# Two heads per tile and batched gathering in a decode attention kernel

## The chip, the cores and the metric

The kernel runs on one core of a Trainium2 chip. The time is device microseconds of that core, from launch to end. Three runs of the kernel before took 393.71, 392.96 and 393.02 us; their median, 393.02 us, is what the change is compared with. A separate profiled execution took 393.22 us; inside it the profile sees 391.4 us from the first to the last instruction (the span).

The core has a matrix engine (TensorE, PE in the profile, with weight loads listed apart as PEld), a vector engine (VectorE, DVE), a scalar engine (ScalarE, ACT), GpSimd (POOL) and a sync engine (SyncE, SP), which here only issues transfers. Sixteen DMA engines move data between the main memory (HBM) and the on-chip memory (SBUF). Matrix products land in a second on-chip memory, PSUM.

## The reference

One token is decoded: `x` is one row of 512 numbers. After a layer norm, two branches run on it and both are added to `x`.

```python
xn = layernorm(x)
# A: attention over a cache of 4096 keys, 32 heads of 128
q = (xn @ wq).reshape(32, 128)
scores = einsum("hd,hkd->hk", q, k_cache) * 128 ** -0.5
p = softmax(scores)
o = einsum("hk,hkd->hd", p, v_cache)
a = o.reshape(4096) @ wo
# B: SwiGLU, 512 -> 1376 -> 512, scaled by a router's sigmoid, plus xn
y = (silu(xn @ w_gate) * (xn @ w_up)) @ w_down * sigmoid(xn @ w_r)
out = x + a + (xn + y)
```

All of it is float32. The two caches hold 32 x 4096 x 128 numbers each, 67.1 MB; `wq` and `wo` are 8.4 MB each and the three matrices of branch B 2.8 MB each. Every weight and cache entry is used once.

## The kernel before

**Loads.** One pool of 12 slots of 128 x 4096 floats (2 MB, 16 KB per partition) takes every weight and cache tile in turn, so a load waits until the tile that held its slot twelve loads earlier has been used up. All of these loads go through SP's queue, in the order `wq` (4 loads), `w_gate`, `w_up` (2 each), K of head 0, then K of head g and V of head g-1 alternately, then `wo` (8 loads of 1 MB) and `w_down` (3 loads and a last one for 96 rows that are left over). One head's keys, 4096 x 128, lie as 128 partitions x 32 keys (chunks) x 128.

**Scores.** Loop round g does head g's scores and the rest of head g-1. Of head g's 32 chunks, VectorE multiplies 12 with the head's query in two bulk instructions (`multiply`, L281), in place, and ScalarE sums each of these chunks with an instruction of its own (`sums`, L288). The other 20 are done by VectorE with a fused multiply-and-sum, one instruction and a read-out of its accumulator per chunk (`dots`, L292). The query has to stand on all 128 partitions; a matrix product with a row of ones copies it there, once per head (`q_group`, L222).

**Softmax and values.** For head g-1, VectorE takes each partition's maximum and spreads it over a diagonal (`own_max`, L299 and L301), TensorE mixes the partitions (L303), VectorE takes the head's maximum (`head_max`, L308) and ScalarE the exponentials with their sums (`expo`, L315). TensorE sums these sums over the partitions (`denominators`, L183), and multiplies exponentials with V: 16 products of 2 chunks each, in four column groups of the array (`values`, L332). ScalarE copies the result out of PSUM (`gather`, L340). Eight products with a selection matrix pick the four column groups' parts, add them, and turn the row of 128 into a column layout (`collect`, L354); ScalarE scales by the inverse of the denominator (L359). Every fourth head VectorE copies the four heads' results to a tile of their own (`keep`, L365).

**Branch B** runs while the first keys arrive: two products with `w_gate` and `w_up` (L238), sigmoid, and 41 small products that turn the hidden row into columns (L267, L269).

**The end.** 172 products (`accumulate`, L372) multiply all heads' results with `wo` and the hidden columns with `w_down`, all into one PSUM tile, in the order of the loads. VectorE adds the residual (L418), and SP stores the row (L419).

The order on every engine is the order in which the code is written; no scheduler moves anything. A float32 matrix product is two passes on TensorE, each with a weight load and a multiplication of its own, so each of the 1152 products in the code gives four instructions (2304 PE and 2304 PEld in the profile).

Of the kernel before, what the change touches and what calls it, by code (L numbers as in the profile page):

```python
# [14 lines left out]
HP = 1  # L15
SLOTS = 12
NA = 12
G = 2
# [3 lines left out]
NJ = 10  # L22


@with_exitstack
def kernel(
# [21 lines left out]
    GB = HB // HP  # L48
# [4 lines left out]
    QC = 512  # L53
    SLOT = C * Dh
    EPS = 1e-5
# [7 lines left out]
    ps_s = ctx.enter_context(tc.tile_pool(name="ps_s", bufs=3, space=bass.MemoryType.PSUM))  # L63
# [3 lines left out]
    def slot(name):  # L67
        return stream.tile([P, SLOT], F32, name="slot")

    def load_wq():  # L70
        rows = SLOT // (H * Dh)
        src = wq.rearrange("(p j) n -> p (j n)", p=P)
        WQ = []
        for i in range(0, NK, rows):
            t = slot("wq")
            nc.sync.dma_start(t, src[:, i * H * Dh:(i + rows) * H * Dh])
            WQ += [t[:, j * H * Dh:(j + 1) * H * Dh] for j in range(rows)]
        return WQ

    def load_in(w):  # L80
        rows = min(NK, SLOT // F)
        src = w.rearrange("(p j) f -> p (j f)", p=P)
        W = []
        for i in range(0, NK, rows):
            t = slot("w_in")
            n = rows * F
            nc.sync.dma_start(t[:, :n], src[:, i * F:i * F + n])
            W += [t[:, j * F:(j + 1) * F] for j in range(rows)]
        return W

    def load_cache(cache, g):
        t = slot("kv")
# [4 lines left out]
    def load_wo():  # L97
        W = []
        n = SLOT // (RB * D)
        for b in range(0, H // HB, n):  # L100
            t = slot("wo").rearrange("p (b r n) -> p b (r n)", b=n, n=D)
# [8 lines left out]
    def load_down():  # L110
        src = w_down[:FM, :].rearrange("(p j) n -> p j n", p=P)
        rows = SLOT // D
        W = []
        if rows > NJ:
            t = slot("w_down").rearrange("p (j n) -> p j n", n=D)
            parts = [(t, 0, 5), (t, 5, 3), (t, 8, 2)]
            last = t[:, NJ]
        else:
            t = slot("w_down").rearrange("p (j n) -> p j n", n=D)
            u = slot("w_down").rearrange("p (j n) -> p j n", n=D)  # L120
            parts = [(t, 0, 5), (u, 0, 3), (u, 3, 2)]
            last = u[:, NJ - 5]
        j = 0
        for t, at, n in parts:
            nc.sync.dma_start(t[:, at:at + n], src[:, j:j + n])
            W += [t[:, at + i] for i in range(n)]
            j += n
        nc.sync.dma_start(last[:FL, :], w_down[FM:, :])
        return W + [last]
# [12 lines left out]
    K, V = {}, {}  # L142
    K[0] = load_cache(k_cache, 0)
# [10 lines left out]
    nc.vector.memset(ps_acc, 0.0)  # L154
    ps_pv = [ps_1.tile([P, 512], F32, name=f"ps_pv{i}") for i in range(2)]
    for t in ps_pv:
        nc.vector.memset(t, 0.0)
# [7 lines left out]
    nc.gpsimd.memset(same, 0.0)  # L165
    for h in range(HP):
        nc.gpsimd.memset(same[h * PP:(h + 1) * PP, h * PP:(h + 1) * PP], 1.0)

    M = G * HP
# [6 lines left out]
    RS = [const.tile([P, HP], F32, name=f"rs{i}") for i in range(2)]  # L176
    for t in (*PT, *RS):
        nc.gpsimd.memset(t, 0.0)


    def total(cols, n=1):
        ps = ps_s.tile([P, 512], F32, name="ps_small")
        nc.tensor.matmul(ps[:, 0:n], ones, cols, start=True, stop=True)  # L183
        return ps[:, 0:n]
# [19 lines left out]
    NB = H * Dh // (QC * NCOL)  # L204
    for j in range(NK):
        for b in range(NB):
            for t in range(NCOL):
                n = (b * NCOL + t) * QC
                nc.tensor.matmul(ps_pv[b][32 * t:32 * t + 1, :], xnT[:, j:j + 1],  # L209
                                 WQ[j][:, n:n + QC], start=(j == 0), stop=(j == NK - 1),  # L210
                                 skip_group_check=True)
    q_sb = const.tile([P, NB, QC], F32, name="q_sb")
    for b in range(NB):
        nc.scalar.activation(q_sb[:, b, :], ps_pv[b], AF.Copy)
# [42 lines left out]
    QG = {0: q_group(0)}  # L257
# [5 lines left out]
    nc.vector.scalar_tensor_tensor(hid, hid, sr, up, op0=ALU.mult, op1=ALU.mult)  # L263
    ps_h = ps_s.tile([P, 512], F32, name="ps_small")
    for j in range(NJ):
        for t in range(NCOL):
            nc.tensor.matmul(ps_h[32 * t:32 * t + 32, j:j + 1], hid[32 * t:32 * t + 1, j:FC:NJ],  # L267
                             ones[32 * t:32 * t + 1, 0:1], start=True, stop=True)
    nc.tensor.matmul(ps_h[:FL, NJ:NJ + 1], hid[0:1, FC:FC + FL], ones[0:1, 0:1],  # L269
                     start=True, stop=True)  # L270
    hT = const.tile([P, NJ + 1], F32, name="hT")
    nc.vector.tensor_copy(hT[:, :NJ], ps_h[:, :NJ])
    nc.vector.tensor_copy(hT[:FL, NJ:], ps_h[:FL, NJ:NJ + 1])
# [174 lines left out]
```

## Time and profile before

| what | value |
|---|---|
| median of three runs | 393.02 us |
| profiled execution, its span | 393.22 us, 391.4 us |
| instructions in the span | 7371 |
| PE, PEld busy | 245.9 us, 126.7 us |
| DVE busy | 278.1 us (71%) |
| ACT busy | 189.5 us (48%) |
| HBM read | 159.46 MB, 407 GB/s over the span |

A row of a group of instructions gives line, engine, operation, output and inputs with their shapes and a count; behind the bar stand the busy time of all of them, the mean of one in ns, and the engine's idle time just ahead of them with what ended it. A row of a table by stretches gives, for each engine, busy us and the number of instructions in the stretch, then TensorE's granted clock (1.00 is full), the mean busy share of the sixteen DMA engines, and what they moved. A row of a DMA queue gives packets, MB and the time that its packets took as a share of sixteen engines' time. In the chain of waits a row is start, duration, and what the end of the program was waiting for then.

### The profile page before, as it was taken

The page shows a single profiled execution, that of the slowest core. Times are in us where ns is not written, and L with a number is a line of the kernel's source. Part 1 is how long each engine was busy: PE and PEld are TensorE (multiplying, and loading weights), DVE is VectorE, ACT ScalarE, POOL GpSimd, SP SyncE. Part 2 cuts the span into 40 slices and gives each one's busy share as a digit, 9 for nine tenths or more (in the row PEclk, how much of TensorE's full clock was granted, in tenths as well). Part 3 has the DMA queues.
Part 4 walks back from the last instruction along what each step waited for, and adds up shares of the span by engine and source line. Part 5 has one row for each costly group of instructions (what it writes and reads, how often), then busy time and mean ns, then how long its engine had stood idle before and what let it go on. Part 6 is the DMA issues. An engine that isn't in the chain of part 4 may idle for free.

```text
span 391.4 us, 7371 instructions
## 1 busy us (share of the span) xinstructions
PE 245.9 (63%) x2304; PEld 126.7 (32%) x2304; DVE 278.1 (71%) x1511; ACT 189.5 (48%) x903; POOL 1.4 (0%) x13
## 2 busy tenths in 40 slices
PE   0745447776666566666665665666656666666854
PEld 0111223343333233333333333333323333333522
DVE  2013599998888888778887887787878877888000
ACT  1020456655555555556554555565545555656000
POOL 1000000000000000000000000000000000000000
PEclk9997655666666565655655555555565655656879
DMA  8999999999999999999999999999999999999960
GB/s 322 425 424 428 425 429 428 423 429 427 427 427 424 429 424 426 429 427 427 424 429 426 425 427 425 429 424 429 426 424 427 427 425 429 427 420 418 422 241 18
DMA packets 12407, 159.93 MB, mean 409 GB/s; under 512 B 1640, under 2 KB 1648, under 8 KB 2000
## 3 DMA queue, kind: packets, MB, share of 16 engines
q1 hardware_dynamic: 12072, 159.46, 96.4%
q8 instruction: 18, 0.29, 0.3%
q14 instruction: 21, 0.17, 0.1%
q10 hardware_dynamic: 296, 0.01, 0.0%
HBM read 159.46 MB, written 0.00 MB: 407 GB/s over the span
## 4 chain that ended last, share of the span: by engine, by line
DMA 92%; PE 3%; ACT 2%; issue 1%; DVE 1%; SPq 0%
DMA slot<-in_A_k_cache_dram 50%; DMA slot<-in_A_v_cache_dram 21%; DMA slot<-in_A_wo_dram 8%; DMA slot<-in_B_w_gate_dram 5%; DMA slot<-in_B_w_down_dram 5%; DMA xT<-in_A_x_dram 2%; PE ps_pv L332 2%; ACT junk L288 1%; PE ps_small L303 1%; PE ps_small L354 0%; ACT pt L315 0%; DVE slot L281 0%; PE ps_acc L372 0%; DVE nm L308 0%; DVE dg L301 0%
## 5 line engine op out<-in xcount | busy, mean ns | idle before, releaser
L292 DVE CUSTOM_DVE_ANT_0 junk<-slot,q 128x128 f32<-128x128 f32 x640 | 183.3, 286 | 21.1
L288 ACT ACTIVATE junk<-slot 128x128 f32<-128x128 f32 x384 | 118.3, 308 | 47.3 <-DVE slot L281 33.4
L332 PE MATMUL ps_pv<-slot,pt 128*2 128x256 f32 x1024 | 113.0, 618 | 16.9 <-DMA slot<-in_A_v_cache_dram 16.9
L281 DVE TENSOR_TENSOR slot<-slot,q 128x768 f32<-128x768 f32 x64 | 60.7, 949 | 18.5 <-issue 11.8
L288 ACT ACTIVATION_READ_ACCUMULATOR junk<-slot 128x1 f32 x384 | 71.6, 186 | 0.0
L332 PEld LDWEIGHTS ps_pv<-slot,pt 128*2 128x2 f32 x1024 | 31.8, 117 | 78.8 <-issue 54.6
L303 PE MATMUL ps_small<-dg,same 128*128 128x128 f32 x64 | 23.0, 457 | 51.4 <-DVE dg L301 51.4
L292 DVE DVE_READ_ACCUMULATOR2_ANT s<- 128x1 f32 x640 | 52.2, 82 | 0.0
L354 PEld LDWEIGHTS ps_small<-sel,pv_sb 128*32 128x32 f32 x512 | 33.2, 155 | 43.9 <-ACT pv_sb L340 43.9
L354 PE MATMUL ps_small<-sel,pv_sb 128*32 128x1 f32 x512 | 35.9, 199 | 16.2 <-ACT pv_sb L340 16.2
L183 PE MATMUL ps_small<-rs,ones 128*128 128x1 f32 x64 | 18.7, 362 | 28.1 <-ACT pt L315 28.1
L303 PEld LDWEIGHTS ps_small<-dg,same 128*128 128x128 f32 x64 | 14.4, 280 | 54.1 <-DVE dg L301 44.4
L183 PEld LDWEIGHTS ps_small<-rs,ones 128*128 128x128 f32 x64 | 16.0, 311 | 36.7 <-ACT pt L315 36.7
L315 ACT ACTIVATE pt<-s,nm 128x32 f32<-128x32 f32 x32 | 10.3, 321 | 35.2 <-DVE nm L308 35.2
L359 ACT ACTIVATE o<-ps_small,rinv 32x4 f32<-32x4 f32 x32 | 8.2, 256 | 38.8 <-PE ps_small L354 38.8
L340 ACT ACTIVATE pv_sb<-ps_pv 128x256 f32<-128x256 f32 x32 | 12.3, 384 | 29.9 <-PE ps_pv L332 29.8
L222 PE MATMUL q<-q_sb,ones 1*128 1x128 f32 x64 | 24.6, 484 | 0.0
L222 PEld LDWEIGHTS q<-q_sb,ones 1*128 1x128 f32 x64 | 15.4, 297 | 0.5
L418 DVE TENSOR_TENSOR res<-base,ps_acc 128x128 f32<-128x128 f32 x1 | 0.3, 286 | 20.3 <-PE ps_acc L372 20.3
L372 PE MATMUL ps_acc<-slot,o 128*1 128x128 f32 x256 | 10.6, 321 | 5.2 <-DMA slot<-in_A_wo_dram 5.2
L209 PE MATMUL ps_pv<-slot,xnT 128*1 128x512 f32 x64 | 8.7, 684 | 5.6 <-DMA slot<-in_A_wq_dram 4.7
L238 PE MATMUL ps_pv<-slot,xnT 128*1 128x320 f32 x64 | 6.8, 558 | 6.7 <-DMA slot<-in_B_w_up_dram 4.0
(65 smaller groups left out, 78.0 us busy)
## 6 DMA issues: line engine op xcount, KB each, us to landing
slot<-in_A_k_cache_dram SPq DMA_DIRECT2D x32, 2048.0 KB, 40.1
slot<-in_A_v_cache_dram SPq DMA_DIRECT2D x32, 2048.0 KB, 40.1
slot<-in_A_wq_dram SPq DMA_DIRECT2D x4, 2048.0 KB, 14.3
slot<-in_A_wo_dram SPq DMA_DIRECT2D x8, 1024.0 KB, 31.7
slot<-in_B_w_gate_dram SPq DMA_DIRECT2D x2, 1376.0 KB, 21.3
slot<-in_B_w_up_dram SPq DMA_DIRECT2D x2, 1376.0 KB, 25.5
slot<-in_B_w_down_dram SPq DMA_DIRECT2D x1, 1280.0 KB, 21.0
slot<-in_B_w_down_dram SPq DMA_DIRECT2D x1, 768.0 KB, 20.4
```

What stands on the lines that cost most here:

```text
L183: nc.tensor.matmul(ps[:, 0:n], ones, cols, start=True, stop=True)
L209: nc.tensor.matmul(ps_pv[b][32 * t:32 * t + 1, :], xnT[:, j:j + 1], WQ[j][:, n:n + QC], start=(j == 0), stop=(j == NK - 1), skip_group_che ...
L222: nc.tensor.matmul(ps[i * PP:(i + 1) * PP, :], ones[32 * t:32 * t + 1, :PP], q_sb[32 * t:32 * t + 1, b, at:at + Dh], start=True, stop=True)
L281: nc.vector.tensor_tensor(K[g][:, c0:c1, :], K[g][:, c0:c1, :], QG[g][:, None, :].to_broadcast([P, c1 - c0, Dh]), op=ALU.mult)
L288: nc.scalar.activation(junk, K[g][:, c, :], AF.Copy, accum_out=S[g][:, c:c + 1])
L292: nc.vector.tensor_tensor_reduce(junk2, K[g][:, c, :], QG[g], 1.0, 0.0, op0=ALU.mult, op1=ALU.add, accum_out=S[g][:, c:c + 1],)
L303: nc.tensor.matmul(ps[:, :PP], same, dg, start=True, stop=True)
L315: nc.scalar.activation(PT[g % 2][r, :, i], s[r, :], AF.Exp, bias=nm[r, :], scale=SCALE, accum_out=RS[g % 2][r, i:i + 1])
L332: nc.tensor.matmul(ps[r:r + M, :G * Dh], p[:, G * i:G * (i + 1), :].rearrange("p c h -> p (c h)"), v[:, G * i:G * (i + 1), :].rearrange("p ...
L340: nc.scalar.activation(t, ps_pv[g % 2][:, :G * Dh], AF.Copy)
L354: nc.tensor.matmul(po[q, r:r + 1], t[:, c * Dh + r:(c + 1) * Dh:RB], sel[:, c * HP + i:c * HP + i + 1], start=(c == 0), stop=(c == G - 1),)
L372: nc.tensor.matmul(ps_acc[32 * j:32 * j + 1, :DC], lhsT, rhs[:, j * DC:(j + 1) * DC], start=first[0], stop=last, skip_group_check=True)
```

## The change

Two heads share a tile: each has 64 partitions, and a tile is 4 MB with 32 KB per partition (64 chunks of 128). The pool has 5 such slots. A loop round now does two heads, so there are 16 rounds.

- The keys' multiplication is done by VectorE alone, for all 64 chunks, in three bulk instructions. ScalarE sums 16 chunks one by one as before, and VectorE sums 48 in one bulk instruction. The fused multiply-and-sum is gone.
- Queries are spread for four rounds (eight heads) in one product.
- `values` takes four chunks per product: 16 products with 512 columns for two heads, where there were 32 with 256.
- The column groups' results are kept for four rounds. Then `collect` does eight heads at once: 4 products for the denominators, 16 that pick and add the column groups, one reciprocal and two scalings on VectorE, and a VectorE transpose of 32 x 32 blocks in place of the turning products. Branch B's 41 turning products are replaced by one such transpose too.
- The last load of `w_down` lies as 32 partitions x 3 rows instead of 96 x 1, which makes three products per column group of it instead of one.

```diff
-HP = 1
-SLOTS = 12
-NA = 12
-G = 2
+HP = 2
+GB = 4
+SLOTS = 5
+NA = 16
+G = 4
...
-        nc.sync.dma_start(last[:FL, :], w_down[FM:, :])
-        return W + [last]
+        nl = FL // T
+        nc.sync.dma_start(t[:T, NJ:NJ + nl], w_down[FM:, :].rearrange("(p j) n -> p j n", p=T))
+        return [t[:, j] for j in range(NJ)] + [t[:T, NJ + j] for j in range(nl)]
...
-    def q_group(g):
-
-        ps = ps_q.tile([P, Dh], F32, name="q")
-        for i in range(HP):
-            n = (g * HP + i) * Dh
-            b, t, at = n // (NCOL * QC), n // QC % NCOL, n % QC
-            nc.tensor.matmul(ps[i * PP:(i + 1) * PP, :], ones[32 * t:32 * t + 1, :PP],
-                             q_sb[32 * t:32 * t + 1, b, at:at + Dh], start=True, stop=True)
+    def q_batch(b):
+
+        ps = ps_q.tile([P, GB, Dh], F32, name="q")
+        r = 32 * (b * HP % NCOL)
+        s = slice(r, r + 32 * HP)
+        nc.tensor.matmul(ps.rearrange("p g d -> p (g d)"), pick[s, :], q_sb[s, b * HP // NCOL, :],
+                         start=True, stop=True)
         return ps
...
+    hT = const.tile([P, NJ + FL // T, T], F32, name="hT")
+    nc.vector.transpose(hT.rearrange("p j i -> p (j i)"), hr)
...
-    def dots(g, c0, c1):
-        for c in range(c0, c1):
-            nc.vector.tensor_tensor_reduce(
-                junk2, K[g][:, c, :], QG[g], 1.0, 0.0, op0=ALU.mult, op1=ALU.add,
-                accum_out=S[g][:, c:c + 1],
-            )
+    def sums_dve(g, c0, c1):
+        nc.vector.tensor_reduce(S[g][:, c0:c1], K[g][:, c0:c1, :], axis=AX.X, op=ALU.add)
...
-                ps[r:r + M, :G * Dh], p[:, G * i:G * (i + 1), :].rearrange("p c h -> p (c h)"),
+                ps[r:r + M, :], p[:, G * i:G * (i + 1), :].rearrange("p c h -> p (c h)"),
...
-    def collect(g, t):
-
-        po = ps_s.tile([P, 512], F32, name="ps_small")
-        rinv = RI.pop(g)
-        for i in range(HP):
-            hl = (g * HP + i) % HB
-            q = slice(32 * hl, 32 * hl + 32)
-            for r in range(RB):
-                for c in range(G):
-                    nc.tensor.matmul(
-                        po[q, r:r + 1], t[:, c * Dh + r:(c + 1) * Dh:RB],
-                        sel[:, c * HP + i:c * HP + i + 1],
-                        start=(c == 0), stop=(c == G - 1),
-                    )
-            nc.scalar.activation(O[g // GB][q, :], po[q, :RB], AF.Copy, scale=rinv[q, i:i + 1])
+    def collect(b):
+
+        pv, rs = PV.pop(b), RS.pop(b)
+        den = ps_s.tile([P, 512], F32, name="ps_small")
+        n = GB // BB
+        for t in range(HB):
+            k, h = t // HP, t % HP
+            nc.tensor.matmul(den[32 * t:32 * t + 32, :BB], same[:, h * PP:h * PP + 32], rs[:, k::n],
+                             start=True, stop=True)
+        for c in range(G):
+            for t in range(HB):
+                k, h = t // HP, t % HP
+                nc.tensor.matmul(ps_o[32 * t:32 * t + 1, :BB * Dh], sel[:, c * HP + h:c * HP + h + 1],
+                                 pv[:, c, k::n, :], start=(c == 0), stop=(c == G - 1),
+                                 skip_group_check=True)
+        rinv = small.tile([P, BB], F32, name="rinv")
+        nc.vector.reciprocal(rinv, den[:, :BB])
+        o = small.tile([P, BB, RB, T], F32, name="o")
+        for i in range(BB):
+            nc.vector.tensor_scalar(
+                o[:, i].rearrange("p r i -> p i r"),
+                ps_o[:, i * Dh:(i + 1) * Dh].rearrange("p (i r) -> p i r", r=RB),
+                rinv[:, i:i + 1], None, op0=ALU.mult,
+            )
+        ot = const.tile([P, BB, RB, T], F32, name=f"ot{b}")
+        nc.vector.transpose(ot.rearrange("p b r i -> p (b r i)"), o.rearrange("p b r i -> p (b r i)"))
+        OT[b] = ot
...
             S[g] = small.tile([P, C], F32, name="s")
-            multiply(g, 0, NA // 2)
-            sums(g, 0, NA // 8)
+            multiply(g, 0, NA)
+            sums_act(g, 0, NA // 4)
...
-            multiply(g, NA // 2, NA)
+            multiply(g, NA, (NA + C) // 2)
         if g:
             head_max(g - 1)
             expo(g - 1)
-            denominators(g - 1)
-        if g + 1 < NG:
-            QG[g + 1] = q_group(g + 1)
+        if g % GB == 0 and g // GB + 1 < NB:
+            Q[g // GB + 1] = q_batch(g // GB + 1)
         if g < NG:
-            dots(g, NA, C)
-            sums(g, NA // 8, NA)
+            multiply(g, (NA + C) // 2, C)
+            sums_act(g, NA // 4, NA)
+            sums_dve(g, NA, C)
         if g:
-            inverse(g - 1)
             values(g - 1)
-            t = gather(g - 1)
-            collect(g - 1, t)
+            keep(g - 1)
             if g % GB == 0:
-                keep(g // GB - 1)
+                collect(g // GB - 1)
```

The first place to look at is VectorE in the loop, where it takes up a new tile of keys. These are the rows before, at the start of a round; the names are the tiles of the code (`slot` a tile of keys, `s` the scores, `m`, `dg` and `nm` the steps of the maximum).

```order
L281 TENSOR_TENSOR slot<-slot,q 128x768
L299 TENSOR_REDUCE m<-s 128x1
L301 TENSOR_SCALAR dg<-fold,m 128x128
L281 TENSOR_TENSOR slot<-slot,q 128x768
L308 TENSOR_REDUCE nm<-ps_small 128x1
L292 ISA junk_297,s<-slot,q 128x128
L292 ISA s 128x1
```

The last two, a fused multiply-and-sum and its read-out, stand there twenty times in a row, followed by the reciprocal. This is one of the four rounds of the change that end with a `collect`, whole.

```order
L272 TENSOR_TENSOR slot<-slot,q 128x2048
L286 TENSOR_REDUCE m<-s 128x1
L288 TENSOR_SCALAR dg<-fold,m 128x64
L272 TENSOR_TENSOR slot<-slot,q 128x3072
L295 TENSOR_REDUCE nm<-ps_small 128x1
L272 TENSOR_TENSOR slot<-slot,q 128x3072
L282 TENSOR_REDUCE s<-slot 128x48
L341 RECIPROCAL rinv<-ps_small 128x2
L344 TENSOR_SCALAR o<-ps_o,rinv 128x32x4 x2
L350 STREAM_TRANSPOSE ot_515<-o 128x256
```

A round of two heads has seven VectorE instructions in place of some ninety, and in every fourth round four more stand between it and the next keys; the first of these needs the round's products with V.

The second place is TensorE's list at the end, from the last products with V on. Before:

```order
L332 MATMUL ps_pv_112<-slot,pt_126 2x256 x16
L354 MATMUL ps_small<-sel,pv_sb 32x1 x8
L372 MATMUL ps_acc<-slot,o_664 1x128 x16
L372 MATMUL ps_acc<-slot,o_995 1x128 x16
...
L372 MATMUL ps_acc<-slot,o_2958 1x128 x16
L372 MATMUL ps_acc<-slot,hT 1x128 x44
```

With the change:

```order
L313 MATMUL ps_pv_104<-slot,pt_128 8x512 x16
L332 MATMUL ps_small<-rs,same 32x2 x4
L337 MATMUL ps_o<-pv,sel 1x256 x16
L357 MATMUL ps_acc<-slot,ot_515 1x128 x32
...
L357 MATMUL ps_acc<-slot,ot_1223 1x128 x32
L357 MATMUL ps_acc<-slot,hT 1x128 x52
```

The products with `wo` stay 128 and still come behind the last heads' results, which now wait for twice as many products with V, for 20 products of `collect` and for the four VectorE instructions above; those with `w_down` are 52 instead of 44. Counted over the whole list, TensorE has 611 products where it had 1152. VectorE's list has 161 instructions where it had 1511, and ScalarE's 311 (256 of them sums and 32 exponentials, each with a read-out behind it) where it had 487.

More of the change, by code (lines that the diff above doesn't have):

```diff
@@ L22 @@
 NJ = 10
+T = 32
 @with_exitstack
@@ L110, in load_down @@
     def load_down():
+        t = slot().rearrange("p (j n) -> p j n", n=D)
         src = w_down[:FM, :].rearrange("(p j) n -> p j n", p=P)
[L112 to L122, printed above, removed]
         j = 0
-        for t, at, n in parts:
-            nc.sync.dma_start(t[:, at:at + n], src[:, j:j + n])
-            W += [t[:, at + i] for i in range(n)]
+        for n in (5, 3, 2):
+            nc.sync.dma_start(t[:, j:j + n], src[:, j:j + n])
             j += n
-        nc.sync.dma_start(last[:FL, :], w_down[FM:, :])
-        return W + [last]
+        nl = FL // T
+        nc.sync.dma_start(t[:T, NJ:NJ + nl], w_down[FM:, :].rearrange("(p j) n -> p j n", p=T))
+        return [t[:, j] for j in range(NJ)] + [t[:T, NJ + j] for j in range(nl)]
     xT = const.tile([P, NK], F32, name="xT")
@@ L153 @@
     ps_acc = ps_1.tile([P, 512], F32, name="ps_acc")
-    nc.vector.memset(ps_acc, 0.0)
+    ps_o = ps_1.tile([P, 512], F32, name="ps_o")
     ps_pv = [ps_1.tile([P, 512], F32, name=f"ps_pv{i}") for i in range(2)]
-    for t in ps_pv:
+    for t in (*ps_pv, ps_o, ps_acc):
         nc.vector.memset(t, 0.0)
@@ L165 @@
     nc.gpsimd.memset(same, 0.0)
+    pick = const.tile([P, P], F32, name="pick")
+    nc.gpsimd.memset(pick, 0.0)
     for h in range(HP):
-        nc.gpsimd.memset(same[h * PP:(h + 1) * PP, h * PP:(h + 1) * PP], 1.0)
-    M = G * HP
+        s = slice(h * PP, (h + 1) * PP)
+        nc.gpsimd.memset(same[s, s], 1.0)
+        for r in range(32 * h, P, 32 * HP):
+            nc.gpsimd.memset(pick[r:r + 1, s], 1.0)
     sel = const.tile([P, M], F32, name="sel")
@@ L175, with total @@
     PT = [const.tile([P, C, HP], F32, name=f"pt{i}") for i in range(2)]
-    RS = [const.tile([P, HP], F32, name=f"rs{i}") for i in range(2)]
-    for t in (*PT, *RS):
+    for t in PT:
         nc.gpsimd.memset(t, 0.0)
-    def total(cols, n=1):
+    def total(col):
         ps = ps_s.tile([P, 512], F32, name="ps_small")
-        nc.tensor.matmul(ps[:, 0:n], ones, cols, start=True, stop=True)
-        return ps[:, 0:n]
+        nc.tensor.matmul(ps[:, 0:1], ones, col, start=True, stop=True)
+        return ps[:, 0:1]
     s1 = const.tile([P, 1], F32, name="s1")
@@ L312, in expo @@
         nm, s = MX.pop(g), S.pop(g)
+        if g % GB == 0:
+            RS[g // GB] = small.tile([P, GB], F32, name="rs")
         for i in range(HP):
@@ L315, in expo @@
             nc.scalar.activation(PT[g % 2][r, :, i], s[r, :], AF.Exp, bias=nm[r, :], scale=SCALE,
-                                 accum_out=RS[g % 2][r, i:i + 1])
-    def denominators(g):
-        RI[g] = total(RS[g % 2], HP)
-    def inverse(g):
-        rinv = small.tile([P, HP], F32, name="rinv")
-        nc.vector.reciprocal(rinv, RI[g])
-        RI[g] = rinv
+                                 accum_out=RS[g // GB][r, g % GB:g % GB + 1])
     def values(g):
```

108 lines of the change are left out of this document (47 added, 61 removed).

## The prediction

> **What bounds the kernel now.** I read the page's time by slices and its DMA queues first, then the chain of waits from its end, then the last 40 us in stretches. The page:
>
> ```profile
> GB/s 322 425 424 428 425 429 428 423 429 427 427 427 424 429 424 426 429 427 427 424 429 426 425 427 425 429 424 429 426 424 427 427 425 429 427 420 418 422 241 18
> ...
> q1 hardware_dynamic: 12072, 159.46, 96.4%
> q8 instruction: 18, 0.29, 0.3%
> q14 instruction: 21, 0.17, 0.1%
> ...
> DMA 92%; PE 3%; ACT 2%; issue 1%; DVE 1%; SPq 0%
> ```
>
> From the second slice to the 38th the loads run at about 427 GB/s, whatever the compute engines do, and 92% of the chain is DMA. The change leaves the 159.46 MB as they are, so faster arithmetic alone buys nothing. But 159.46 MB at 427 GB/s are 373 us, and the last two slices (19.6 us) move next to nothing. The chain's end, and the last stretches:
>
> ```profile
> 368.46 19.19 DMA slot<-in_B_w_down_dram
> ...
> 387.69 0.92 PE ps_acc L372 x24
> 388.61 0.02 issue
> 388.63 0.29 DVE res L418
> ```
>
> ```profile
> 362.00:374.00 12.00, 9.21 (x199) 6.02 (x202) 0.34 (x2) 0.96 (x4) 0.00 (x0) 0.86 1.01 420
> 374.00:376.00 2.00, 0.51 (x20) 0.21 (x8) 0.00 (x0) 0.00 (x0) 0.00 (x0) 1.00 0.93 316
> 376.00:378.00 2.00, 1.43 (x28) 0.99 (x32) 0.00 (x0) 0.00 (x0) 0.00 (x0) 0.52 0.63 252
> 378.00:380.00 2.00, 1.44 (x32) 0.69 (x24) 0.00 (x0) 0.00 (x0) 0.00 (x0) 0.50 0.35 128
> 380.00:382.00 2.00, 1.34 (x32) 0.64 (x24) 0.00 (x0) 0.00 (x0) 0.00 (x0) 0.50 0.12 48
> 382.00:384.00 2.00, 1.25 (x28) 0.69 (x20) 0.00 (x0) 0.00 (x0) 0.00 (x0) 0.77 0.06 26
> 384.00:386.00 2.00, 1.27 (x40) 0.94 (x40) 0.00 (x0) 0.00 (x0) 0.00 (x0) 1.00 0.06 27
> 386.00:388.00 2.00, 1.14 (x36) 0.82 (x40) 0.00 (x0) 0.00 (x0) 0.00 (x0) 1.00 0.08 29
> ```
>
> The next-to-last column is the busy share of sixteen DMA engines. Up to 374 us all work; then they finish one after another, and from 382 us a share of 0.06, one sixteenth, is left: a single engine at 27 GB/s, which is 427/16. The last load lands at 368.46 + 19.19 = 387.65 us because that engine is late. Evenly spread, the rest would have been through at 374 + 2 x (0.93+0.63+0.35+0.12+0.06+0.06+0.08) = 378.5 us: **9.2 us of the time are one engine's lag.**
>
> What that engine had more to do stands in the queues. The loads give all sixteen alike (128 partitions). The two instruction queues move 0.46 MB beside them. q8's 0.29 MB over the 4608 PE and PEld instructions are 63 bytes each, q14's 0.17 MB over the 2414 of DVE and ACT 70: so q8 looks like TensorE's code and q14 the others'. If one DMA engine carries all of q8, it has 0.29 MB / 26.7 GB/s = 10.9 us more to do, and an even share of all code would be 0.46/16 MB, 1.1 us. The difference, 9.8 us, fits the 9.2 us seen.
>
> **The change part by part. Code loading:** TensorE's list shrinks from 1152 to 611 products, four instructions each, so q8 goes from 18 packets to 9.5. 8.5 packets of 0.29/18 = 0.0161 MB at 26.7 GB/s are 5.1 us; by the lag seen, 9.2 x 8.5/18 = 4.3 us. VectorE and ScalarE go from 1511 + 903 instructions to 161 and some 600 with the read-outs; with q14 halved, at the least, the even share falls by (0.137 + 0.085)/16 MB, 0.5 us. Together -4.8 to -5.6; I take **-5.6**, since the bytes explain the lag, with the ends 0 (the lag has another cause) and -9.7 (it goes wholly).
>
> The Trainium skill ("Runtime: NRT & Kernel Launch", Instruction fetch mechanics) has code come in blocks of 16 KiB over the sequencer's own DMA queue, as the 18 packets of 0.016 MB do here, and calls a block's cost mostly hidden. That holds for the engine that executes it, and speaks against a price; what the sum would be then is the first rival below.
>
> **Packets.** Key, value, `wq` and gate/up rows double to 32 KB per partition. No row shows a packet of that size. The nearest: 16 KB rows run at 427 GB/s in mid-program, the 8 KB rows of `wo` at 420 (362 to 374 us). Doubling bought 1.7%; if that is a fixed cost per packet, the next doubling buys 0.8% of the 148 MB concerned, 148/0.427 x 0.008 = 2.8 us. It may buy nothing (0), or lose as much as the weakest stretch below does, 425 for 427, 1.7 us. I take **-1.3**, between the first two, as nothing in the rows points to a loss.
>
> The Trainium skill ("DMA: Bandwidth & Descriptors", Specifications) gives 435 GB/s as the fabric's ceiling; by it packets of any size could give at most 2%, 7 us, and the sum above stays below that.
>
> **VectorE in the loop**, from these groups and one mid-program stretch:
>
> ```profile
> L292 DVE CUSTOM_DVE_ANT_0 junk<-slot,q 128x128 f32<-128x128 f32 x640 | 183.3, 286 | 21.1
> L288 ACT ACTIVATE junk<-slot 128x128 f32<-128x128 f32 x384 | 118.3, 308 | 47.3 <-DVE slot L281 33.4
> L332 PE MATMUL ps_pv<-slot,pt 128*2 128x256 f32 x1024 | 113.0, 618 | 16.9 <-DMA slot<-in_A_v_cache_dram 16.9
> L281 DVE TENSOR_TENSOR slot<-slot,q 128x768 f32<-128x768 f32 x64 | 60.7, 949 | 18.5 <-issue 11.8
> L288 ACT ACTIVATION_READ_ACCUMULATOR junk<-slot 128x1 f32 x384 | 71.6, 186 | 0.0
> ...
> L292 DVE DVE_READ_ACCUMULATOR2_ANT s<- 128x1 f32 x640 | 52.2, 82 | 0.0
> ```
>
> ```profile
> L308 DVE TENSOR_REDUCE nm<-ps_small 128x1 f32<-128x128 f32 x32 | 9.3, 290 | 1.3 <-PE ps_small L303 0.6
> L301 DVE TENSOR_SCALAR dg<-fold,m 128x128 f32<-128x128 f32 x32 | 9.2, 287 | 1.1
> ...
> L299 DVE TENSOR_REDUCE m<-s 128x1 f32<-128x32 f32 x32 | 5.7, 179 | 0.0
> ...
> L231 DVE RECIPROCAL hid<-hid 128x416 f32<-128x416 f32 x1 | 2.8, 2753 | 0.0
> ...
> L214 ACT ACTIVATE q_sb<-ps_pv 128x512 f32<-128x512 f32 x2 | 1.2, 598 | 13.5 <-PE ps_pv L209 13.5
> ...
> L195 DVE TENSOR_REDUCE s<-sq 128x1 f32<-128x4 f32 x1 | 0.2, 157 | 0.0
> ```
>
> ```profile
> 250.00:290.00 40.00, 26.80 (x216) 14.10 (x216) 33.79 (x186) 23.09 (x113) 0.00 (x0) 0.53 1.00 425
> ```
>
> Two heads are 8.39 MB, 19.65 us of loading: the period that VectorE must keep. Before it was busy 33.79 of 40 us, 16.6 per period. Now: a reduction costs (290 - 157)/124 = 1.07 ns per element on 0.15 us, so the 48 x 128 elements 6.7 us. With the same fixed part the multiplication has (949 - 153)/768 = 1.04 ns: 2048, 3072 and 3072 elements, 9.0 us. The three small ones were 0.76 us with twice the width (L299, L301, L308). That makes 16.5 us, 3.2 under the period: worth 0 while that cover stands. ScalarE has 16 x (308 + 186) = 7.9 us of sums and two exponentials, far below it. For TensorE, 32 multiplications of 256 columns now become as many of 512 per round.
>
> Every fourth round VectorE waits in `collect`, with the next keys' multiplication queued behind. Quotable for products with V, and for the end of the program, are these rows (start, duration, group):
>
> ```profile
> 362.87 3.35 PE L332 MATMUL ps_pv<-slot,pt 128*2 128x256 f32 x32
> ...
> 370.98 1.05 PE L372 MATMUL ps_acc<-slot,o 128*1 128x128 f32 x32 [0.48 <-DMA slot<-in_A_wo_dram]
> ...
> 376.57 1.89 PE L372 MATMUL ps_acc<-slot,o 128*1 128x128 f32 x32 [2.06 <-DMA slot<-in_A_wo_dram]
> ```
>
> V of the round before lands half a period after the keys, 9.8 us; 6.7 us of products (twice 3.35), a copy of 0.6 (L214), some 4 us of `collect` products (an estimate: 40 instructions, 32 of them with 256 columns, at the pace of those above) bring that to 21 us, so VectorE loses 5 us and 1.5 of its own four times. The transposes are in no row: between a copy's 0.2 us and what the costliest row allows (the reciprocal of the hidden row, 128x416 in 2753 ns, so 1.7 us for 256 elements). The next two rounds give it back.
>
> **Slots** hide all that. Issues of key tiles, with their count, size and median us to landing, before:
>
> ```profile
> slot<-in_A_k_cache_dram SPq DMA_DIRECT2D x32, 2048.0 KB, 40.1
> ```
>
> So eight loads were under way (8 x 4.9 us). Now a tile of keys occupies its slot for some 17 us after landing while four other loads of 9.8 us, 39 us, keep the engines fed: 22 us of cover, less the collect's 6. If it were gone, every us over would be paid once per round.
>
> **The end.** Behind the last landing stood 24 multiplications, 0.92 us; the leftover rows now make 24 instead of 8, 40 in all: +0.6 us at the same pace. The residual and the store stay.
>
> **Sum:** -5.6 - 1.3 + 0.6 = -6.3 us on the profiled execution's 393.22, 386.9; that one lay 0.2 above the median, so **386.7 us**. Its own range is 385.2 (packets at -2.8) to 390.5 (code at -4.8, packets at +1.7).
>
> **Rivals.** *The lag has another cause*, say one DMA engine that is slower than the rest: for it, that no row names the engine of a packet, and the page's share for q8, 0.3% of 16 x 391.4 us, 19 us, is not the 9.2. Against it: at 27 GB/s the last engine is as fast as the average one. Then -1.3 + 0.6 remain, 392.3; without the gain of packets 393.6. Chance 0.13.
>
> *TensorE becomes the end.* The last V lands 11.2 MB (26.3 us) before the last load, at 380.8 - 26.3 = 354.5; values, copy, collect and VectorE's part (1.6) bring it to some 368, and only then come 256 multiplications with `wo`, 8.4 us at the pace of the rows above, in time. At half the clock the same 32 took 1.89 us (376.57, clock 0.52); then 256 and the 104 of `w_down` take 21.3 us, to 389.3, and the end comes 2.8 us later (391.4 - 388.6 before): a span of 392.1, so 393.7 and no change. It decides from 1.2 times the full-clock pace on, where 11.8 us of work no longer end with the loads. Against it: the stretch from 362 to 374 us had a clock of 0.86 under the same kind of steady work. Chance 0.08.
>
> The Trainium skill ("TensorE: Matmul & The Clock Gate", What's actually happening) has the gate open after some 3.4 us of steady activity; from 354.5 us on TensorE would be active enough, and the trace's 0.86 agrees.
>
> *VectorE becomes the bound, slower.* The bulk sum has 48 rows; if each starts anew, at the 0.15 us that a small reduction has as its fixed part, it takes 6.7 + 48 x 0.15 = 13.9 us, the round 23.7 in place of 19.65, and sixteen rounds 65 us more: about 450. It decides once the sum takes over 9.9 us. For it: no row reduces more than one line per partition. Against it: the bulk multiplication, which runs through six lines with a repeated query, shows nothing of it (1.04 ns per element). Chance 0.06.
>
> *Long rows load worse*, or five slots run dry, by a per cent or two: 391 to 398. For it only that neither is in the trace. Chance 0.05.
>
> **How the numbers follow.** The forecast has 0.68. Faster by over 0.2% (below 392.2; about what a measurement of this kernel can tell from no change) are the forecast, half of the case of another cause (0.06) and half of TensorE's end (0.04): 0.78. Within 0.2%: 0.10, the rest of these two but a little. Slower: 0.12, the last two and that little. The range reaches down to a lag that goes wholly (-9.7 - 1.3 + 0.6, 382.6) and up over the case of another cause, most of TensorE's end and the forecast's own range, to 393.2; what it leaves out is VectorE's bound and most of the long rows.
>
> **What would show it.** q8 at 9 to 10 packets; after the drop from full share, a single engine's stretch of some 5 us instead of 10; the last load landing near 381 us; mid-program above 427 GB/s; `multiply` at 2.3 and 3.3 us, the bulk sum near 6.7; VectorE's waits at `collect` with no hole in the loads. Wrong is the main step if q8 halves and the lag stays, or if the loads' rate falls anywhere before the last 15 us.

## The result, and the profile after

The changed kernel takes 383.65 us (four runs, 383.55 to 384.7) against 393.12 us for the kernel before beside it: a ratio of 0.9762, 95% interval 0.9743 to 0.9782, so 9.5 us or 2.4% faster. Its span is 381.8 us, where 391.4 stood. A second measurement gave 0.9759 (0.974 to 0.9777).

From the page of the changed kernel, the rate of the loads by slices, the queues, and the chain's shares:

```profile
GB/s 330 440 414 449 439 433 409 433 429 439 433 439 426 411 426 439 439 438 433 422 423 424 439 436 433 436 422 427 426 438 439 429 436 423 429 426 406 419 414 81
...
q1 hardware_dynamic: 6824, 159.45, 97.8%
q8 instruction: 9, 0.15, 0.2%
...
q14 instruction: 9, 0.07, 0.0%
...
DMA 75%; DVE 16%; PE 4%; issue 3%; ACT 1%; SPq 1%; DVEq 0%
```

The loads run without a hole from the second slice to the 39th, and a little faster than before. DVE has 16% of the chain because a slot of keys is now given back by the bulk sum, and the chain walks back through that; the loads were not waiting for it, as the rates show.

The last stretches of the changed kernel, columns as before:

```profile
370.00:372.00 2.00, 1.88 (x32) 0.98 (x32) 0.00 (x0) 0.00 (x0) 0.00 (x0) 0.50 0.98 405
372.00:374.00 2.00, 0.69 (x16) 0.49 (x20) 0.00 (x0) 0.00 (x0) 0.00 (x0) 0.50 0.84 286
374.00:376.00 2.00, 2.00 (x44) 1.12 (x40) 0.00 (x0) 0.00 (x0) 0.00 (x0) 0.50 0.37 127
376.00:378.00 2.00, 1.77 (x47) 0.88 (x43) 0.00 (x0) 0.00 (x0) 0.00 (x0) 0.70 0.04 15
```

and the end of its chain of waits:

```profile
357.51 19.66 DMA slot<-in_B_w_down_dram
377.17 0.04 issue
377.22 1.42 PE ps_acc L357 x40
378.66 0.29 DVE res L400
```

The last landing moved from 387.65 to 377.17 us, by 10.5. (These are the landings of the last load over all 128 partitions; the leftover rows follow 0.4 to 0.5 us behind, while its products run.) Counted as in the prediction, an even finish would have been at 372 + 2 x (0.84+0.37+0.04) = 374.5 us, where it was 378.5. So **the lag of the last DMA engine fell from 9.2 to 2.7 us (6.5), the even finish came 4.0 us earlier, and the work behind the last landing grew by 0.5 us** (0.92 to 1.42). From the residual to the end of the span it is 3.1 us, 0.3 more than before. VectorE's groups:

```profile
L272 DVE TENSOR_TENSOR slot<-slot,q 128x3072 f32<-128x3072 f32 x32 | 107.0, 3346 | 0.0
L282 DVE TENSOR_REDUCE s<-slot 128x48 f32<-128x6144 f32 x16 | 104.8, 6553 | 0.5
...
L272 DVE TENSOR_TENSOR slot<-slot,q 128x2048 f32<-128x2048 f32 x16 | 36.6, 2286 | 41.0 <-DMA slot<-in_A_k_cache_dram 41.0
...
L344 DVE TENSOR_SCALAR o<-ps_o,rinv 128x128 f32<-128x128 f32 x8 | 2.8, 426 | 7.8 <-PE ps_o L337 7.8
L350 DVE STREAM_TRANSPOSE ot<-o 128x256 f32<-128x256 f32 x4 | 1.8, 445 | 0.1
...
L341 DVE RECIPROCAL rinv<-ps_small 128x2 f32<-128x2 f32 x4 | 0.7, 162 | 7.6 <-PE ps_small L332 7.6
```

The bulk sum is 6.55 us and the three multiplications 2.29 and 2 x 3.35. VectorE waits 41 us in all for keys, so it keeps up; the four `collect` stages cost it 15.4 us of waiting, which reaches no load.

### The profile page after: what moved, and what is told of

It reads as the page before. It is cut to its first block, busy times and chain, and to the rows that moved or that the text cites. A ratio compares the mean times of both kernels' runs of the same rounds, so it can differ in the third digit from the quotient of the medians.

```text
span 381.8 us, 3430 instructions
## 1 busy us (share of the span) xinstructions
PE 152.2 (40%) x1222; PEld 45.6 (12%) x1222; DVE 270.4 (71%) x161; ACT 131.2 (34%) x599; POOL 2.2 (1%) x17
## 4 chain that ended last, share of the span: by engine, by line
DMA 75%; DVE 16%; PE 4%; issue 3%; ACT 1%; SPq 1%; DVEq 0%
DMA slot<-in_A_k_cache_dram 53%; DMA slot<-in_A_v_cache_dram 9%; DVE slot L272 8%; DMA slot<-in_A_wo_dram 8%; DVE s L282 7%; DMA slot<-in_B_w_down_dram 5%; PE ps_pv L313 3%; ACT junk L279 1%; PE ps_acc L357 0%; SPq L90 0%; DVE dg L288 0%; DVE m L286 0%; ACT pt L304 0%; SPq L80 0%; SPq L105 0%
## 5 line engine op out<-in xcount | busy, mean ns | idle before, releaser
L272 DVE TENSOR_TENSOR slot<-slot,q 128x3072 f32<-128x3072 f32 (+1 forms) x48 | 143.5, 2993 | 41.0 <-DMA slot<-in_A_k_cache_dram 41.0
L313 PE MATMUL ps_pv<-slot,pt 128*8 128x512 f32 x512 | 92.0, 885 | 90.1 <-DMA slot<-in_A_v_cache_dram 79.3
L279 ACT ACTIVATE junk<-slot 128x128 f32<-128x128 f32 x256 | 79.2, 310 | 107.1 <-DVE slot L272 99.7
L282 DVE TENSOR_REDUCE s<-slot 128x48 f32<-128x6144 f32 x16 | 104.8, 6553 | 0.5
L290 PE MATMUL ps_small<-dg,same 128*128 128x64 f32 x32 | 10.7, 436 | 109.4 <-DVE dg L288 109.4
L279 ACT ACTIVATION_READ_ACCUMULATOR junk<-slot 128x1 f32 x256 | 47.7, 186 | 0.0
L313 PEld LDWEIGHTS ps_pv<-slot,pt 128*8 128x8 f32 x512 | 16.7, 116 | 155.2 <-ACT junk L279 84.3
L304 ACT ACTIVATE pt<-s,nm 64x64 f32<-64x64 f32 x32 | 11.2, 350 | 33.3 <-DVE nm L295 33.1
L357 PE MATMUL ps_acc<-slot,ot 128*1 128x128 f32 x256 | 10.3, 307 | 4.2 <-DMA slot<-in_A_wo_dram 3.5
L337 PE MATMUL ps_o<-pv,sel 128*1 128x256 f32 x128 | 10.0, 378 | 1.0 <-ACT pv L322 1.0
```

Of the source, the lines that this page charges most:

```text
L272: nc.vector.tensor_tensor(K[g][:, c0:c1, :], K[g][:, c0:c1, :], q[:, None, :].to_broadcast([P, c1 - c0, Dh]), op=ALU.mult)
L279: nc.scalar.activation(junk, K[g][:, c, :], AF.Copy, accum_out=S[g][:, c:c + 1])
L282: nc.vector.tensor_reduce(S[g][:, c0:c1], K[g][:, c0:c1, :], axis=AX.X, op=ALU.add)
L290: nc.tensor.matmul(ps[:, :PP], same, dg, start=True, stop=True)
L304: nc.scalar.activation(PT[g % 2][r, :, i], s[r, :], AF.Exp, bias=nm[r, :], scale=SCALE, accum_out=RS[g // GB][r, g % GB:g % GB + 1])
L313: nc.tensor.matmul(ps[r:r + M, :], p[:, G * i:G * (i + 1), :].rearrange("p c h -> p (c h)"), v[:, G * i:G * (i + 1), :].rearrange("p c d - ...
```

## The experiments

Three explanations stood against each other. **The prediction's**: TensorE's code, loaded by one DMA engine, is the lag. **S**: the lag goes with the number and size of the loads. **V**: it is the code of VectorE and ScalarE. Packet length was to be settled apart from them. For each load the trace has the sixteen times at which a DMA engine reported its share; this is how the reports of a load at the end lay behind the first one in ten of the kernels (us), with what the kernels issue. In the rows from the kernel before, the load is the leftover rows of `w_down`; in the others it is the one ahead of that, the last over all 128 partitions:

```
kernel             products  VectorE  ScalarE | median  last but one  last
before                 1152     1511      487 |    3.0           6.0  12.0
before_less_pe          640     1511      487 |    1.8           6.1  12.2
before_more_pe         1600     1511      487 |    4.6           5.7  11.9
before_part_bulk       1152     1255      487 |    3.2           5.8  10.0
before_bulk            1152      295      487 |    3.8           5.7   6.2
after                   611      161      311 |    2.1           3.5   4.4
pe_code                1155      161      311 |    3.3           4.2   4.7
vec_code                611      561      791 |    1.5           5.8   7.1
more_act                611      161      631 |    1.6           2.8   5.1
fewer_act_sums          611      161      183 |    2.1           3.0   3.5
```

(ScalarE's sums and exponentials have a read-out each beside the counted instruction.) The other one of the two loads gives 12.5, 12.5, 12.3, 10.3 and 6.4 us in the last column for the first five rows and 4.2, 4.5, 6.6, 5.0 and 3.5 for the others, so the choice moves it by 0.5 us at most. This column is from the first engine; the 9.2 and 2.7 us above are from an even finish.

### TensorE's code

**pe_code**: the changed kernel with idle products.

```diff
+        if g:
+            for _ in range(34):
+                nc.tensor.matmul(ps_acc[0:1, 300:301], ones[:, 0:1], ones[:, 0:1], start=True, stop=True,
+                                 skip_group_check=True)
         if g < NG:
             multiply(g, (NA + C) // 2, C)
```

> The changed kernel with 34 products of one column per round that nothing uses, so that TensorE has about as many products as before the change (1155); loads, slots and the other engines stay. Theory (TensorE's code, loaded by one DMA engine, is the lag): the code queue goes from 9 to 18 packets, the lag from 2.7 us to between 8.2 us (0.61 us per packet, by bytes) and 9.2 us, the even finish by 0.3 us, the time to 389.1 to 390.4 us. Rivals S (loads) and V (code of VectorE and ScalarE): no change, 383.7 us.

Measured: 384.95 us (ratio to before 0.9791, 0.9775 to 0.9807), 1.0 to 1.3 us slower than the changed kernel, not 5.5 to 6.5. The queues of this kernel:

```profile
q8 instruction: 18, 0.29, 0.3%
...
q14 instruction: 8, 0.07, 0.0%
```

q8 is TensorE's code, as had been worked out: it doubled. But the last engine stayed near where it was, 4.7 us behind the first where it had been 4.4.

**before_less_pe**: the kernel before with fewer products.

```diff
-        ng = C // G
+        ng = NCOL
...
-                for c in range(G):
+                for c in range(1):
...
-                        start=(c == 0), stop=(c == G - 1),
+                        start=True, stop=True,
```

> The kernel before with TensorE's code cut: of each head's 16 products with V only the first 4 are done, and of its 8 selecting products 4 (three quarters of the values and half of the selected parts are left out of the result). TensorE has 640 products instead of 1152; tiles, loads and slots stay. Theory: the code queue goes from 18 to 10 packets, the lag from 9.2 us down by 4.1 to 5.8 us, the even finish stays, time 387.3 to 389.0 us. Rivals S and V: 393.1 us.

Measured: 393.54 us, ratio 1.0003 (0.9993 to 1.0012): no change. Its queues and two of its last stretches:

```profile
q8 instruction: 10, 0.16, 0.2%
q14 instruction: 21, 0.17, 0.1%
```

```profile
384.00:386.00 2.00, 1.27 (x40) 0.94 (x40) 0.00 (x0) 0.00 (x0) 0.00 (x0) 1.00 0.06 27
386.00:388.00 2.00, 1.18 (x39) 0.83 (x40) 0.00 (x0) 0.00 (x0) 0.00 (x0) 1.00 0.09 29
```

Eight packets of TensorE's code less, and the single late engine is still there, to the same microsecond.

**before_more_pe**: 14 such idle products per head in the kernel before, at the same place.

```diff
+        if g:
+            for _ in range(14):
+                nc.tensor.matmul(ps_acc[0:1, 300:301], ones[:, 0:1], ones[:, 0:1], start=True, stop=True,
+                                 skip_group_check=True)
         if g < NG:
             dots(g, NA, C)
```

> The kernel before with 14 products of one column more per head (448 in all, 1792 instructions) that nothing uses. Theory (TensorE's code is the lag): 7 packets more of code, the lag grows from 9.2 us by 3.6 to 5.0 us, time 396.7 to 398.1 us. Rivals S and V: 393.1 us, unless TensorE itself becomes too slow, which would show as loads that stop in mid-program.

Measured: 393.38 us, ratio 0.9999 (0.999 to 1.0009), with 25 packets in q8. The prediction's explanation is false. The table shows where TensorE's code does go: the median of the engines moves with it, 1.8, 3.0 and 4.6 us for 10, 18 and 25 packets, so it is spread over many engines, none of them the last.

### VectorE's code

**vec_code**: the changed kernel with idle instructions on VectorE and ScalarE.

```diff
             sums_dve(g, NA, C)
+            for _ in range(25):
+                nc.vector.memset(idle_v, 0.0)
+            for _ in range(30):
+                nc.scalar.activation(idle_a, eps_t, AF.Copy)
...
```

> The changed kernel with 25 tiny VectorE and 30 tiny ScalarE instructions more per round, 880 in all, that nothing uses. Theory (only TensorE's code makes the lag): the lag stays within 0.5 us, time 383.7 to 384.3 us. Rival V (the code of VectorE and ScalarE makes the lag): of the 1350 VectorE instructions and some 300 of ScalarE that the change took away, half are back, so half of the lag is: time about 387 us.

Measured: 391.74 us (0.9959, 0.9945 to 0.9974), 8 us slower than the changed kernel and more than V had forecast. Part of it is something else, as VectorE's groups, the end of the chain and a stretch show:

```profile
L390 DVE MEMSET idle_v<- 128x1 f32 x400 | 23.6, 59 | 25.3
```

```profile
368.26 5.99 PE ps_pv L315 x31
374.33 0.61 ACT pv L324
374.98 1.58 PE ps_o L339 x25
376.77 10.07 PE ps_acc L359 x355
```

```profile
380.00:382.00 2.00, 2.00 (x84) 1.83 (x78) 0.00 (x0) 0.00 (x0) 0.00 (x0) 1.00 0.03 8
```

400 idle instructions take 23.6 us busy and as much again between them (59 ns and a gap of 63), 3.1 us per round: the whole of VectorE's slack. It waits 2.9 us in all for keys, where it waited 41 in the changed kernel, so a delay is not made up. The last products with V begin at 368.3 us (350.2 in the changed kernel), and TensorE goes on after the loads have ended. ScalarE has a part in it: its idle instructions stand ahead of the copies that `collect` needs, and take 6.2% of the chain. So the 8 us are compute that is late, and the run's time does not tell V's price. What does speak for V is the table: the last engine is 7.1 us behind instead of 4.4, the last but one 5.8 instead of 3.5. V was therefore made sharper, as **theory D**: VectorE's code, 8 KB for 128 instructions, falls on one DMA engine and makes the 12 us; ScalarE's falls on another and makes the 6 us of the last but one. It was tried in the kernel before, where nothing else of the change is present.

**before_bulk**: bulk form instead of the fused one, in the kernel before.

```diff
         if g < NG:
-            dots(g, NA, C)
+            multiply(g, NA, C)
+            nc.vector.tensor_reduce(S[g][:, NA:C], K[g][:, NA:C, :], axis=AX.X, op=ALU.add)
```

> The kernel before with the fused multiply-and-sum replaced by the change's bulk form: VectorE multiplies all 32 chunks of a head and sums 20 of them in one instruction; tiles of one head, 12 slots, loads and TensorE's 1152 products stay. Theory D (VectorE's code, in packets of 8 KB on one DMA engine, is the lag of 12 us against the first engine, 1.0 us per packet; ScalarE's on another one is the 6 us of the second slowest): VectorE's list falls from 1511 to 295 instructions, 12 packets to 2, so ScalarE's 6 us are left, the last load lands 6 us earlier, time 386.9 to 388.0 us. The theory of the prediction (TensorE's code) and theory S (size and number of loads): 393.4 us.

Measured: 387.14 us, ratio 0.9839 (0.9825 to 0.9854), 6.2 us faster than the kernel before, with tiles, loads, slots and 18 packets of TensorE's code as they were. Its queues and last stretches:

```profile
q8 instruction: 18, 0.29, 0.3%
q14 instruction: 12, 0.10, 0.1%
```

```profile
376.00:378.00 2.00, 0.60 (x16) 0.50 0.62 250
378.00:380.00 2.00, 2.00 (x40) 0.50 0.35 122
380.00:382.00 2.00, 1.97 (x40) 0.50 0.10 35
382.00:384.00 2.00, 0.65 (x20) 0.95 0.00 0
```

(This table is of TensorE alone: busy us, granted clock, DMA share, GB/s.) Up to 382 us the shares are those of the kernel before, 0.63, 0.35 and 0.12; then there is nothing left where it had one engine for 6 us more. VectorE has hardly less to do in this kernel (32.8 us of 40 on the mean from 90 to 330 us, 33.3 before), so it is not its time that counts.

**before_part_bulk**: the same for 5 of 20 chunks.

```diff
-            dots(g, NA, C)
+            dots(g, NA, C - 5)
+            multiply(g, C - 5, C)
+            nc.vector.tensor_reduce(S[g][:, C - 5:C], K[g][:, C - 5:C, :], axis=AX.X, op=ALU.add)
```

> The same for 5 of the 20 chunks only: 1255 VectorE instructions, 10 packets instead of 12. Theory D: the last engine's lag falls by 2.0 to 2.5 us, time 390.7 to 391.5 us. If it is not the number of instructions but the fused form as such: a quarter of what the whole replacement brings, 391.8 us. Theory of the prediction and S: 393.4 us.

Measured: 391.47 us, ratio 0.9956 (0.994 to 0.9973), 1.9 us faster. The last engine went from 12.0 to 10.0, one us per packet of 128 instructions, and its last landing (366.38 + 19.13 us in the chain) from 387.65 to 385.5. The time alone does not tell the number of instructions from the fused form (391.8 was forecast for the latter); the landing speaks for the number.

The trace of the kernel before has it packet by packet. It gives the time of each q14 packet but not its DMA engine, so the lag is followed from load to load here. Up to the load that lands at 96.7 us, the last report is at most 2.1 us behind the first one. Then (packet's start, and the last report's lag in the loads that land behind it, us):

```
q14 packet   101  125  152  182  206  234  263   287   315   344
lag          3.1  4.1  5.0  6.0  7.0  7.9  9.0  10.0  11.0  11.9
```

Between these packets the lag stays; each adds about 1.0 us to it. They come some 27 us apart, the time in which VectorE gets through 128 instructions (46 per head of 9.8 us). Most of the other q14 packets come some 42 us apart, near ScalarE's pace (28 instructions per head, so 45 us for 128), and at those from 188 us on, where it can be followed, the last engine but one goes up by about 0.7 us each. A packet of q8 sets one engine back by about 1.5 us, and another one each time. In vec_code both kinds of step are seen: the last engine (7.1) goes up by 0.7 us some 38 us apart, ScalarE's pace there, and the last but one (5.8) by 1.0 at 208, 288 and 368 us, VectorE's. So the 7.1 is ScalarE's code, and packets that are mostly VectorE's plain memsets set their engine back by as much as those of the fused form. Whose packet it is is read from the pace, as no row names it.

### ScalarE's code

**fewer_act_sums**: the changed kernel with fewer sums on ScalarE.

```diff
-NA = 16
+NA = 8
```

> The changed kernel with 8 instead of 16 chunks of a round summed one by one on ScalarE, and 56 instead of 48 in VectorE's bulk sum. Theory D: ScalarE's engine is now the last one (4.4 us behind the first); 256 instructions fewer are 2 packets, 1.5 us, and the next engines are at 3.5 and 3.0, so the last load lands 0.9 to 1.4 us earlier, time 382.5 to 383.1 us; VectorE has 1.1 us per round more to do, inside its 3 us. Theory of the prediction: 383.9 us. It goes the other way if VectorE's smaller slack keeps it behind the loads to the end.

Measured: 383.92 us, ratio 0.9751 (0.973 to 0.9772): no change to be told. The last engine is 0.9 us less behind, but the end of its chain shows where that went:

```profile
353.82 21.09 DMA slot<-in_B_w_down_dram
374.91 0.04 issue
374.95 3.87 PE ps_acc L357 x64
```

TensorE takes 60 ns for each of its last 64 multiplications, where the last 40 of the changed kernel took 36; the granted clock is 0.50 from 372 to 380 us, where the changed kernel had 0.70 and 1.00 in its last two stretches. They end at 378.8, as late as in the changed kernel.

**more_act**: idle ScalarE instructions in the changed kernel.

```diff
             keep(g - 1)
+            for _ in range(20):
+                nc.scalar.activation(idle_a, eps_t, AF.Copy)
...
```

> The changed kernel with 20 tiny ScalarE instructions per round that nothing uses, 320 in all, put where ScalarE waits for the next keys; VectorE stays. Theory D: 2.5 packets more on ScalarE's DMA engine, 0.75 us each, the last load lands 1.5 to 2.3 us later, time 385.4 to 386.2 us. Theory of the prediction: 383.9 us.

Measured: 383.53 us, ratio 0.9744 (0.9728 to 0.976): no change, a miss. The last engine is 5.1 us behind instead of 4.4, which is in the direction of theory D and a third of its size, while the first engine finished 1.7 us earlier than in the changed kernel. Why the loads as a whole ran faster there isn't shown. So no time confirms theory D for ScalarE. The loads in mid-program do in part: the last engine's lag goes from 2.2 to 2.8, 3.4, 3.9 and 4.5 us at the q14 packets at 188, 237, 277 and 321 us, which are ScalarE's by their pace (56 instructions per round), so a packet of its code costs its engine some 0.6 us.

### Packet length and the end

**half_rows**: the changed kernel with loads of half a row.

```diff
-        nc.sync.dma_start(t, src.rearrange("(p c) d -> p (c d)", p=P))
+        src = src.rearrange("(p c) d -> p (c d)", p=P)
+        for n in range(0, SLOT, SLOT // 2):
+            nc.sync.dma_start(t[:, n:n + SLOT // 2], src[:, n:n + SLOT // 2])
```

> The changed kernel, with each load of keys and values split into two loads of half a row (16 KB per partition instead of 32), nothing else. Theory (longer packets carry the part of the gain that the lag does not): the loads' even finish moves from 374.5 us back by 3.0 to 3.6 us, the lag of the last engine stays at 2.7 us, the time is 386.6 to 387.3 us. Rival S (the lag fell because there are fewer and larger loads, not because of code): the lag grows back towards 9 us too, time 390 us or more. If packet length is worth nothing: 383.7 us.

Measured: 387.28 us, ratio 0.9842 (0.9828 to 0.9857); the changed kernel's second measurement is 383.94, so 3.3 us slower, as forecast. One mid-program stretch of this kernel, then the same of the changed one:

```profile
250.00:290.00 40.00, 16.35 (x108) 3.71 (x108) 32.45 (x19) 15.81 (x74) 0.00 (x0) 0.62 1.01 428
```

```profile
250.00:290.00 40.00, 15.71 (x108) 4.13 (x108) 32.37 (x17) 15.82 (x74) 0.00 (x0) 0.62 1.01 432
```

The lag stayed (4.7 us from the first engine, 4.4 before), so S is out: twice as many loads of half the size bring no lag back.

**before_half_rows**: the same edit in the kernel before, 8 KB rows.

> The kernel before with each load of keys and values split into two loads of half a row, 8 KB per partition instead of 16. Theory (a fixed cost per packet): the rate in mid-program falls from 427 to 420 GB/s, the rate of the 8 KB rows of wo, the even finish moves from 378.5 us by some 5 us, the lag stays, time about 398 us. If packet length is worth nothing: 393.1 us.

Measured: 399.23 us, ratio 1.0142 (1.0127 to 1.0157), 5.8 us slower. The last engine is 13.0 us behind the first, 12.0 before, so the loss is in the rate, here in mid-program:

```profile
250.00:290.00 40.00, 26.57 (x208) 13.17 (x212) 33.58 (x185) 22.69 (x111) 0.00 (x0) 0.50 1.01 420
```

So 8, 16 and 32 KB per packet load at 420, 427 and 429 to 433 GB/s. The length of a row and the size of a load (1, 2 and 4 MB) go together in these runs; that it is the packet is seen in the packets' own times in mid-program, 314.5, 616.6 and 1219 ns on the mean: two short ones take 12 and 14 ns more than one of twice the length. For keys and values, 14 ns on 4096 packets over sixteen engines make 3.6 us (3.3 measured), and 12 ns on 8192 packets 6.3 us (5.8 measured).

**after_again** is the changed kernel, for comparison.

> The changed kernel once more, on the chip of the three that go with it, so that they are compared with it there: 383.5 to 384.0 us.

Measured: 383.94 us, ratio 0.9759.

**short_end**: the leftover rows of `w_down` first, then 5, 4 and 1 rows.

```diff
-        for n in (5, 3, 2):
+        nl = FL // T
+        nc.sync.dma_start(t[:T, NJ:NJ + nl], w_down[FM:, :].rearrange("(p j) n -> p j n", p=T))
+        for n in (5, 4, 1):
...
-        nl = FL // T
-        nc.sync.dma_start(t[:T, NJ:NJ + nl], w_down[FM:, :].rearrange("(p j) n -> p j n", p=T))
...
```

> The changed kernel with the loads of w_down in another order: the leftover rows first, then 5, 4 and 1 rows per partition, so that one row and 8 multiplications stand behind the last landing instead of 40. Theory: what follows the last landing falls from 1.42 to about 0.35 us, time 382.6 to 382.9 us. Rival: the end is covered by the store or by the landing of smaller packets, no change.

Measured: 384.74 us, ratio 0.9773 (0.9759 to 0.9788): not faster. The end of its chain:

```profile
357.52 20.28 DMA slot<-in_B_w_down_dram
377.80 0.04 issue
377.84 2.35 PE ps_acc L357 x40
```

The 4 rows and the single one came so close together that 40 multiplications still stood behind the landing, and TensorE took 59 ns for each, at a granted clock of 0.50 (376 to 380 us).

None of these kernels is faster than the changed one by more than the measurements can tell.

## Why the prediction was right or wrong

**Right: where the time was to be found.** The kernel is bound by its loads, 9.2 us of one DMA engine's work lay behind an even finish, and the change brings its gain there, not in arithmetic. Fewer VectorE instructions alone, in the kernel before (before_bulk), are worth 6.2 of the 9.5 us.

**Wrong: whose code it is.** The step that failed is "q8 looks like TensorE's code ... If one DMA engine carries all of q8, it has ... 10.9 us more to do". The first half holds (q8 doubled with pe_code), the second does not: q8 is spread, and 8 packets fewer or 7 more leave the last engine at 12.2 and 11.9 us. It goes with VectorE's number of instructions, some 12 packets of 8 KB at 1.0 us each, and in the kernel before it grows packet by packet. That the forecast came near is luck in this term: the sum fitted only because bytes over rate for q8 (9.8 us) happened to be near the lag seen (9.2); VectorE's 12 packets at their transfer time would be 12 x 0.0082 MB / 26.7 GB/s = 3.7 us, which made that queue look harmless. Of the signs that the prediction named, q8's halving could not tell, since the change shortens both lists at once; the single engine's stretch could, as it was some 1 us where 5 were put. The rule that a block's cost is mostly hidden (the Trainium skill, "Runtime: NRT & Kernel Launch", Instruction fetch mechanics) agrees with TensorE's code in the kernel before, where 8 packets fewer and 7 more gave 1.0003 and 0.9999 of the time. It does not fit VectorE's, which costs time, though by the loads and not on the engine that runs it. The term came out at -6.5 of lag where -5.1 was put, and the change takes away nearly all VectorE code where only half of TensorE's went.

**Mis-sized: packets.** -1.3 was taken between 0 and -2.8; half_rows measures -3.3. The row used was right (420 to 427 for the first doubling, confirmed by before_half_rows), and the upper end, a fixed cost per packet halved again, was nearly the truth; the cut to half of it had no row behind it. With the 0.5 us that the prediction had for the even share of code, this makes up the 4.0 us of the even finish but for 0.2. The rate of 435 GB/s that the Trainium skill gives ("DMA: Bandwidth & Descriptors", Specifications) was not passed over a longer stretch: those of 40 us reach 433. (Single slices of the page scatter from 406 to 449.)

**Right: the rest of the sum.** The end grew by 0.5 us (0.6 put). The multiplications took 2.29 and 3.35 us (2.3 and 3.3), the bulk sum 6.55 (6.7), a transpose of 256 elements 0.45, nearer the lower bound (0.2) than the upper (1.7). VectorE's wait at `collect`, 15.4 us in four rounds against some 20, cost no load.

In all -9.5 against -6.4: outside the forecast's own range, inside the full one, by two terms that each fell short. (On the span: -6.5 of lag, -4.0 of even finish, +0.5 at the end and +0.3 behind it, -9.7.)

**The rivals.** "The lag has another cause" was nearest to the truth, though not as one slow engine: it was another queue's code, which the change takes away too. "VectorE becomes the bound" did not come, and vec_code fits the margin of 3.2 us per round that had been worked out: with 3.1 us more, and ScalarE's idle instructions beside it, the kernel is 8 us slower. "TensorE becomes the end" did not come in the changed kernel: the last products with V began at 350.2 us, and the clock was 1.00 from 355 to 366 us. From 368 to 376 us it was 0.50, and TensorE is the next bound: in fewer_act_sums the last products ran at half the clock and ate the 0.9 us that the loads had gained, and in short_end 40 of them took 2.35 us where they had taken 1.42. Long rows load better, not worse, and five slots never ran dry.

## What to carry to other kernels

When a kernel is bound by loads, look at how the DMA engines finish, not only at their mean rate: a stretch at one sixteenth of the full share (0.06 here, for 6 us) is one engine still at work, and the time ends with it. Instructions are loads too, and many small ones on VectorE can cost time that VectorE itself never shows as busy or waiting. Which queue is to blame has to be tried by changing one engine's instruction count alone; two numbers that agree are not yet a cause.

## What the runs showed of the hardware that was not expected

A packet of 8 KB of VectorE's code holds up its DMA engine by about 1.0 us, and one of ScalarE's by 0.6 to 0.7. The same bytes of data take 0.31 us, and the q14 packets' own times are 0.31 to 0.42 in the kernel before, so most of the delay is not the transfer itself; what it is stays open. TensorE's code, with packets twice that size, spreads over many engines, about 1.5 us on one engine for a packet, and moved the time by at most 1.3 us for nine packets (pe_code), by none in the kernel before. Beyond 16 KB per packet the loads still gain: 427 to some 431 GB/s. An idle VectorE memset of one column takes 122 ns of the engine, 59 of them busy.
